# Attention and a squared-ReLU MLP on one core: the moving operand of both MLP products read as two interleaved halves

## The chip, the core and the metric

The kernel runs on one core of a Trainium2 chip. The metric is device time in microseconds (us) of one execution, lower is better. A core has TensorE (PE, matrix products, with its weight loads shown apart as PEld), VectorE (DVE), ScalarE (ACT), GpSimd (POOL), SyncE (SP, here the issuer of nearly all DMAs), an on-chip memory of 128 partitions (SBUF), and the accumulator memory that TensorE writes (PSUM).

## The reference

Causal attention over a window of 128 positions with a linear bias per head, for 8 batches, 8 heads, 576 positions and a head size of 64. Its output, 4608 tokens of 512 features, goes through a two-layer mixture with squared ReLU:

```python
scores = scale * np.matmul(q, k.transpose(0, 1, 3, 2))
scores = np.where(mask, scores + bias[None], -1000000000.0)
attn = softmax(scores)                       # window of 128, causal
x = np.matmul(attn, v).transpose(0, 2, 1, 3).reshape(4608, 512)
h = np.maximum(x @ w_in, 0.0)                # w_in  512 x 2048
out = (h * h) @ w_out                        # w_out 2048 x 512
```

Inputs and outputs are float32.

## The kernel before

**Tiles.** The 4608 tokens are worked on in 9 chunks (`NCH`) of 512. Everything is held transposed: features in the 128 partitions, the chunk's 512 tokens in the columns. The hidden layer's 2048 features are 16 blocks (`NF`) of 128.

**Precision.** Products run in fp32r, a four-byte type of fewer significant bits, and each float32 operand is split into a high and a low part. A product is three matmuls: high weight by high data, high weight by low data, low weight by high data.

**First product, `gemm1(c, f)`, L202.** For chunk c and hidden block f it accumulates 4 input blocks by 3 parts, 12 matmuls of 128 x 128 weights by 512 columns, into one PSUM bank `g`. The moving operand is `xs[cc][:, part]`: a row of 512 words of the tile `xu` ([128, 2, 512], high and low parts), which attention wrote. Then ACT takes the ReLU out of PSUM (L212), DVE (in chunk 0 mostly ACT) squares it (L215, L217), ACT rounds it to the high part `hh` (L219), and DVE subtracts to get the low part `hl` (L221). `hh` and `hl` are [128, 512] each.

**Second product, `gemm2(c, f)`, L231.** For hidden block f it adds to the four accumulators `acc` (one per 128 output features) 3 matmuls each, 12 in all, with `hh` and `hl` as moving operands. After the last f the accumulators are copied (L237) and stored (L238) to a transposed output [512, 4608], which the host transposes back.

**Weights.** They stay in SBUF for the whole run. Each high and low word lie side by side (`self.w[f]` is [128, 2, 512, 2]), so the 128 columns of a weight block are read 8 bytes apart. For the first product, in the blocks f = 0, 4, 8, 12 and there in the first two of the four input blocks (`APART`, L39 and L188), the columns are read 16 bytes apart instead; those are 6 of the 12 loads of such a group.

**Order.** From chunk 1 on, a written-out loop (L811 to L834) alternates one `gemm1` and, two hidden blocks behind, one `gemm2`; every eight half-steps the matmuls of the next pair of attention heads (`visit`, L541 and L548) come in between. The order on PE is the program's own. In the start and chunk 0 a planner (`Plan`) orders all engines. Before the first products PE also runs matmuls of zeros in bf16 (L129), whose result nobody uses.

Of the kernel before, what the change touches and what calls it, by code (L numbers as in the profile page):

```python
# [19 lines left out]
B, H, S, D = 8, 8, 576, 64  # L20
NP = H // 2
DM, DF = 512, 2048
NF = DF // 128
NCC = DM // 128
NCH = B * S // 512
# [31 lines left out]

def slope(h):
    return 2.0 ** (-8.0 * (h + 1) / H)


class Kern:
# [131 lines left out]
    def gemm1(self, c, f):  # L194
        nc = self.nc
        xs = [self.x[c, p] for p in range(NP)]
        g = self.big.tile([128, 2, 512], F32, name="g")[:, 1] if self.big else self.g1.tile([128, 512], F32, name="g")
        i = 0
        for cc in range(NCC):
            wl, wh = self.block(0, f, cc)  # L200
            for w, part in ((wh, 0), (wh, 1), (wl, 0)):
                nc.tensor.matmul(g, w, xs[cc][:, part], start=i == 0, stop=i == 11)  # L202
                i += 1
                if (c, f, i) == (0, 0, 9):
                    yield
        yield
        r = self.hp.tile([128, 512], F32, name="r", bufs=1)
        hh = self.hp.tile([128, 512], F32R, name="hh")
        hl = self.hp.tile([128, 512], F32R, name="hl")
        self.h[c, f] = hh, hl  # L210
        with self.tc.high_priority(offset=100):
            self.relu = nc.scalar.activation(r, g, AF.Relu)  # L212
        yield
        if c or f in SQUARES:
            nc.vector.tensor_tensor(r, r, r, op=ALU.mult)  # L215
        else:
            nc.scalar.activation(r, r, AF.Square)  # L217
        yield
        nc.scalar.copy(hh, r)  # L219
        yield  # L220
        nc.vector.tensor_tensor(hl, r, hh.bitcast(F32), op=ALU.subtract)  # L221

    def gemm2(self, c, f):
        nc = self.nc
        hh, hl = self.h.pop((c, f))
        if f == 0:
            self.acc = self.start_banks if c == 0 else [self.ac.tile([128, 512], F32, name="acc") for _ in range(4)]
        for m in range(4):
            wl, wh = self.block(1, f, m)
            for i, (w, h) in enumerate(((wh, hh), (wh, hl), (wl, hh))):  # L230
                nc.tensor.matmul(  # L231
                    self.acc[m], w, h, start=(f == 0 and i == 0), stop=(f == NF - 1 and i == 2)
                )
            if f == NF - 1:
                o = self.op.tile([128, 512], F32, name="o")
                out = self.outd[m * 128 : m * 128 + 128, 512 * c : 512 * c + 512]
                (nc.scalar.copy if m % 2 else nc.vector.tensor_copy)(o, self.acc[m])  # L237
                (nc.scalar if c == NCH - 1 and m == 3 else nc.sync).dma_start(out, o)  # L238
# [598 lines left out]
def _consts():  # L837
    r = np.arange(128)
    own, h = r % 64, (r // 64)[:, None]
    cst = np.zeros((128, CST), np.float32)  # L840
    cst[:, 0:128] = np.eye(128)
    keep = own[:, None] >= np.arange(64)[None, :]
    cst[:, 128:192] = np.where(h == 0, keep, ~keep).astype(np.int32).view(np.float32)
    cst[:, 192:256] = NEG
    rel = r[:, None] - r[None, :]
    rel = np.where(rel >= 0, rel, rel + 128)
    for a in range(H):
        cst[:, 256 + 128 * a : 384 + 128 * a] = -rel * (8 * slope(a))
    later = r[:, None] < r[None, :]
    near = [cst[:, 256 + 128 * a : 384 + 128 * a] for a in range(H)]  # L850
    return np.concatenate([cst] + [np.where(late, t, np.float32(NEG)) for t in near for late in (later, ~later)], axis=1)
# [40 lines left out]
```

## Time and profile before

| what | value |
|---|---|
| median of 3 runs (lowest to highest) | 941.89 us (941.58 to 941.97) |
| the profiled execution's span, first to last instruction | 939.1 us |
| matmuls of L202 / L231 | 1728 / 1728 |
| mean latency of one such matmul | 394 / 393 to 396 ns |
| DMA traffic over the span | 95.26 MB, mean 101 GB/s |

The page of a profile lists the busy time of each engine, a strip of 40 equal slices of the span (a digit is the busy share in tenths; PEclk is the granted TensorE clock), the chain of work that ended last followed back from the last instruction, and the costliest groups of instructions. A row of the groups reads: line, engine, operation, out<-in by the program's names, shape, count, then busy time in us and mean ns of one, then the idle time ahead of them and who ended it. A row of the timeline reads: start in us, length in us, engine, line, operation, and the count of instructions merged into it. A row of one line's view has minimum/median/maximum in ns. Matmuls are pipelined and overlap one another, so the length of one is not what it adds to the span.

### The profile page before, as it was taken

The numbers are of one execution on the slowest core, as the hardware profiler recorded it, in microseconds if no ns is written. First come the engines' busy times: TensorE is split into PE (matmuls) and PEld (weight loads), VectorE is DVE, ScalarE is ACT, GpSimd is POOL, SyncE is SP. The second block draws the span as 40 slices with busy tenths as digits, with TensorE's granted clock in tenths as the row PEclk, the third lists the DMA queues.
The fourth block names the chain that finished last, engine by engine and source line by source line (L and its number), as shares of the span: only waits on it lengthen the run. The fifth ranks groups of instructions, "written<-read, shape, count | busy, mean of one in ns | idle before, by whom it ended". The sixth has DMA issues, their size and how long they took to land.

```text
span 939.1 us, 19485 instructions
## 1 busy us (share of the span) xinstructions
PE 929.3 (99%) x7492; PEld 782.5 (83%) x7492; DVE 497.2 (53%) x1326; ACT 418.9 (45%) x1115; POOL 214.2 (23%) x255
## 2 busy tenths in 40 slices
PE   8899999999999999999999999999999999999998
PEld 5688888888888888888888888888888888888886
DVE  5999874445554555544555444455455454433222
ACT  7898753343444444334434343344444444322222
POOL 4223331222221222222222222221221222220000
PEclk9999999999999999999999999999999999999999
DMA  9975424222432233222423233334322231111001
GB/s 344 403 284 167 135 74 130 71 62 83 129 86 85 78 104 107 64 84 79 125 86 86 73 106 82 86 85 127 88 77 83 75 93 43 38 46 45 1 0 45
DMA packets 72893, 95.26 MB, mean 101 GB/s; under 512 B 8032, under 2 KB 41952, under 8 KB 72800
## 3 DMA queue, kind: packets, MB, share of 16 engines
q1 hardware_dynamic: 72368, 93.36, 32.6%
q8 instruction: 59, 0.97, 0.4%
q10 hardware_dynamic: 432, 0.66, 0.2%
q14 instruction: 34, 0.28, 0.1%
HBM read 67.76 MB, written 26.21 MB: 100 GB/s over the span
## 4 chain that ended last, share of the span: by engine, by line
PE 94%; DMA 3%; DVE 1%; ACT 1%; issue 0%; SPq 0%; POOLq 0%; DVEq 0%
PE acc L231 43%; PE g L202 42%; PE s L541 5%; PE g L548 2%; DMA raw<-in_dram 2%; PE s L548 1%; DMA wide<-in_dram 1%; PE at L346 1%; ACT t L470 0%; PE s L412 0%; PE at L412 0%; DVE t L482 0%; DVE tw L613 0%; DVE pp L629 0%; DVE raw L175 0%
## 5 line engine op out<-in xcount | busy, mean ns | idle before, releaser
L202 PE MATMUL g<-xu,w 128*128 128x512 f32 x1728 | 423.9, 394 | 1.4 <-issue 0.8
L202 PEld LDWEIGHTS g<-xu,w 128*128 128x128 f32 x1728 | 344.6, 209 | 56.7 <-issue 1.7
L231 PE MATMUL acc<-hh,w 128*128 128x512 f32 x1152 | 385.6, 396 | 0.0
L231 PEld LDWEIGHTS acc<-hh,w 128*128 128x128 f32 x1152 | 224.0, 194 | 45.5 <-issue 5.3
L212 ACT ACTIVATE r<-g 128x512 f32<-128x512 f32 x144 | 86.1, 598 | 353.2 <-PE g L202 353.1
L215 DVE TENSOR_TENSOR r<-r 128x512 f32<-128x512 f32 x129 | 91.9, 713 | 255.8 <-ACT r L212 255.8
L231 PE MATMUL acc<-hl,w 128*128 128x512 f32 x576 | 226.2, 393 | 0.0
L334 POOL TENSOR_SCALAR_AFFINE_SELECT pp<-pp 128x512 f32<-128x512 f32 x128 | 112.5, 879 | 215.6 <-DMA pp<-way 139.4
L221 DVE TENSOR_TENSOR hl<-r,hh 128x512 fp32r<-128x512 f32 x144 | 117.6, 816 | 74.4 <-ACT hh L219 71.9
L270 POOL TENSOR_TENSOR t<-t,nm 128x512 f32<-128x512 f32 x64 | 76.1, 1190 | 262.0 <-DVE nm L267 231.4
L231 PEld LDWEIGHTS acc<-hl,w 128*128 128x128 f32 x576 | 112.1, 195 | 19.6
L219 ACT CAST hh<-r 128x512 fp32r<-128x512 f32 x144 | 89.2, 619 | 78.0 <-DVE r L215 76.4
L259 ACT ACTIVATE t<-t,nm 128x128 f32<-128x128 f32 x256 | 100.1, 394 | 11.8 <-DVE nm L252 11.7
L321 DVE STREAM_TRANSPOSE pp<-t 128x512 f32<-128x512 f32 x64 | 45.2, 707 | 47.0 <-POOL t L270 39.5
L252 DVE CUSTOM_DVE_ANT_0 t<-t,cst 128x128 f32<-128x128 f32 x256 | 59.5, 295 | 1.0
L541 PE MATMUL s<-pp,v 64*64 64x128 f32 (+1 forms) x1792 | 52.0, 248 | 0.1
L541 PEld LDWEIGHTS s<-pp,v 64*64 64x64 f32 x1792 | 40.5, 134 | 10.4 <-issue 10.0
L259 ACT ACTIVATION_READ_ACCUMULATOR t<-t,nm 128x1 f32 x256 | 48.6, 190 | 0.0
L482 DVE COPY_PREDICATED t<-cst,s 64x256 f32<-64x256 int32 x100 | 44.4, 444 | 6.0 <-ACT t L463 3.1
L472 POOL MEMSET t<- 64x128 f32 (+1 forms) x44 | 10.0, 228 | 117.8 <-PE s L548 110.5
L529 ACT CAST xu<-s 128x512 fp32r<-128x512 f32 x28 | 16.4, 587 | 41.6 <-DVE t L482 26.6
L470 ACT COPY t<-g 64x256 f32<-64x256 f32 (+2 forms) x86 | 28.0, 340 | 3.8 <-PE g L548 1.0
(71 smaller groups left out, 482.3 us busy)
## 6 DMA issues: line engine op xcount, KB each, us to landing
raw<-in_dram SPq DMA_DIRECT2D x32, 512.0 KB, 8.7
way<-pp SPq DMA_DIRECT2D x256, 64.0 KB, 2.0
pp<-way SPq DMA_DIRECT2D x64, 256.0 KB, 2.8
qk<-in_dram SPq DMA_DIRECT2D x32, 320.0 KB, 3.2
v<-in_dram SPq DMA_DIRECT2D x32, 320.0 KB, 3.9
qk<-in_dram SPq DMA_DIRECT2D x38, 256.0 KB, 4.3
out_dram<-o SPq DMA_DIRECT2D x35, 256.0 KB, 2.6
v<-in_dram SPq DMA_DIRECT2D x3, 256.0 KB, 5.2
```

The costliest lines, as they stand in the source:

```text
L202: nc.tensor.matmul(g, w, xs[cc][:, part], start=i == 0, stop=i == 11)
L212: self.relu = nc.scalar.activation(r, g, AF.Relu)
L215: nc.vector.tensor_tensor(r, r, r, op=ALU.mult)
L219: nc.scalar.copy(hh, r)
L221: nc.vector.tensor_tensor(hl, r, hh.bitcast(F32), op=ALU.subtract)
L231: nc.tensor.matmul(self.acc[m], w, h, start=(f == 0 and i == 0), stop=(f == NF - 1 and i == 2))
L252: self.nc.vector.tensor_tensor_reduce(self.t[:, m], self.t[:, m], self.K.nrel(2 * self.p + m // 2), -0.125, BIG, ALU.add, ALU.min, self.nm ...
L259: return self.nc.scalar.activation(self.t[:, m], self.t[:, m], AF.Exp, bias=nm[:, m : m + 1], scale=-1.0, accum_out=nm[:, 4 + m : 5 + m],)
L270: self.nc.gpsimd.tensor_tensor(self.t, self.t, self.nm[:, 8:12].unsqueeze(2).to_broadcast([128, 4, 128]), op=ALU.mult)
L321: nc.vector.transpose(squares.rearrange("p b m c -> p m b c"), self.t.rearrange("p m (b c) -> p m b c", c=32))
L334: nc.gpsimd.affine_select(to, self.own, pattern=[[-32 * sign, 4], [0, 4], [-sign, 32]], compare_op=op, fill=0.0, base=0, channel_multiplie ...
L541: made.append(mm(to, w, x, start=first and n < 2, stop=not first, skip_group_check=True))
```

## The change

A helper `in_turn` gives a view of a row of 512 words in which its two halves come in turn: word 0, word 256, word 1, word 257, and so on. Both products read their moving operand through it. The result of a matmul is written to PSUM in contiguous order as before, so its column 2b + a holds what was column 256a + b. The tokens of a chunk are thus permuted once by the first product and once more by the second, and the host undoes the permutation twice after the run.

The instructions of every engine, their number, shapes and order, stay as they were; the access pattern of the moving operand in the two matmul lines is what differs.

```diff
+def in_turn(x):
+    return x.rearrange("p (a b) -> p b a", a=2)
...
-                nc.tensor.matmul(g, w, xs[cc][:, part], start=i == 0, stop=i == 11)
+                nc.tensor.matmul(g, w, in_turn(xs[cc][:, part]), start=i == 0, stop=i == 11)
...
                 nc.tensor.matmul(
-                    self.acc[m], w, h, start=(f == 0 and i == 0), stop=(f == NF - 1 and i == 2)
+                    self.acc[m], w, in_turn(h), start=(f == 0 and i == 0), stop=(f == NF - 1 and i == 2)
                 )
...
-    return np.ascontiguousarray(r.results[0]["out_0_dram"].T)
+    out = r.results[0]["out_0_dram"].T
+    for _ in range(2):
+        out = out.reshape(NCH, 256, 2, DM).transpose(0, 2, 1, 3).reshape(B * S, DM)
+    return np.ascontiguousarray(out)
```

## The prediction

> **What bounds the kernel now.** I read the page's busy times first, then the chain of work that ended last, then the costliest groups, and last the timeline of single matmul groups.
>
> ```profile
> span 939.1 us, 19485 instructions
> PE 929.3 (99%) x7492; PEld 782.5 (83%) x7492; DVE 497.2 (53%) x1326; ACT 418.9 (45%) x1115; POOL 214.2 (23%) x255
> PEclk9999999999999999999999999999999999999999
> PE 94%; DMA 3%; DVE 1%; ACT 1%; issue 0%; SPq 0%; POOLq 0%; DVEq 0%
> PE acc L231 43%; PE g L202 42%; PE s L541 5%; PE g L548 2%; DMA raw<-in_dram 2%; PE s L548 1%; DMA wide<-in_dram 1%; PE at L346 1%; ACT t L470 0%; PE s L412 0%; PE at L412 0%; DVE t L482 0%; DVE tw L613 0%; DVE pp L629 0%; DVE raw L175 0%
> L202 PE MATMUL g<-xu,w 128*128 128x512 f32 x1728 | 423.9, 394 | 1.4 <-issue 0.8
> L231 PE MATMUL acc<-hh,w 128*128 128x512 f32 x1152 | 385.6, 396 | 0.0
> L231 PE MATMUL acc<-hl,w 128*128 128x512 f32 x576 | 226.2, 393 | 0.0
> ```
>
> TensorE is busy for 929.3 of 939.1 us, the clock is granted in full throughout, and the two lines that the change edits hold 85% of the chain. They issue 1728 + 1152 + 576 = 3456 matmuls of 512 columns. The mean of one, 394 ns, is a latency; matmuls overlap, so the price is the pitch from one start to the next. I take it from a stretch in which both products alternate without a gap:
>
> ```profile
> 902.05 2.92 PE L202 MATMUL g<-xu,w 128*128 128x512 f32 x12
> 904.81 0.39 PE L231 MATMUL acc<-hh,w 128*128 128x512 f32 x1
> ...
> 907.58 2.97 PE L202 MATMUL g<-xu,w 128*128 128x512 f32 x12
> 910.38 0.39 PE L231 MATMUL acc<-hh,w 128*128 128x512 f32 x1
> ```
>
> Twelve matmuls take 904.81 − 902.05 = 2.76 us, a pitch of **0.230 us**. The second group takes 2.80 us; it is one of the 36 groups (f divisible by 4, nine chunks) whose first six weight loads come through the strided blocks of L188. The other 288 − 36 = 252 groups are plain. So the two products fill 252 × 2.76 + 36 × 2.80 = 796.3 us, and 939.1 − 796.3 = 142.8 us of the span is something else (the start, attention's matmuls between the groups, the last copy and store). The median of the timed runs, 941.89 us, is 2.8 us above this profile's span; I add these 2.8 us at the end.
>
> Whether longer matmuls are absorbed anywhere is seen in the windows by stage:
>
> ```profile
> 0.00:43.00 43.00, 38.46 (x380) 24.83 (x380) 31.38 (x110) 35.09 (x103) 15.07 (x20) 1.00 0.98 371
> 43.00:140.00 97.00, 96.17 (x646) 80.79 (x641) 85.66 (x189) 75.89 (x170) 31.54 (x34) 1.00 0.54 176
> 140.00:905.00 765.00, 764.31 (x6342) 651.35 (x6341) 371.82 (x1017) 300.65 (x831) 167.58 (x201) 1.00 0.28 80
> 905.00:939.10 34.10, 30.38 (x132) 25.52 (x131) 8.30 (x12) 7.26 (x12) 0.00 (x0) 1.00 0.08 31
> ```
>
> The first number after the length is PE. From 43 us, where the products are under way, to 905 us PE idles 0.83 + 0.69 us, about 1.5 us in all. There is nothing to absorb a longer pitch: what one matmul gains or loses is paid 3456 times, on the path.
>
> **The change, part by part.** No instruction is added, removed or moved on any engine, no DMA, and no wait. The relu, square, cast and subtract between the products run over contiguous 512-word rows as before; that their columns mean other tokens costs them nothing, and the host's reordering is outside the metric. Nothing changes in the weight loads, and PSUM is written in the same contiguous order. The whole change is the order in which TensorE reads its moving operand: today word 0, 1, 2, ... of a row, afterwards word 0, 256, 1, 257, ..., so no two words read in succession are neighbours; they lie 1024 bytes apart. The sum has one unknown, the pitch p of such a matmul: time = 142.8 + 2.8 + 3456 × p.
>
> No matmul of this trace streams a strided moving operand, so p must be bounded from the nearest rows. Those are weight loads, which read SBUF too, in three spacings:
>
> ```profile
> L581 PEld LDWEIGHTS acc<-qk x24: 182/186/187, 6.4 to 15.1; 64*128 64x128 f32 x24
> L299 PEld LDWEIGHTS acc<-pp,v x84: 132/137/137, 16.6 to 30.7; 128*64 128x64 f32 x84
> L202 PEld LDWEIGHTS g<-xu,w x12: 193/194/197, 901.8 to 904.4; 128*128 128x128 f32 x12
> ...
> L202 PEld LDWEIGHTS g<-xu,w x12: 193/252/312, 907.3 to 909.9; 128*128 128x128 f32 x12
> ```
>
> The columns are minimum/median/maximum in ns. 128 neighbouring words take 186 (L581), 64 take 137 (L299): (186 − 137)/64 = 0.77 ns a word and 186 − 128 × 0.77 = 88 ns fixed. Words 8 bytes apart (L202, plain group: high and low parts lie in pairs) take 194, hardly more. Words 16 bytes apart, in the six strided loads of the group at 907, take 312. So two words within 16 bytes still come at the contiguous price, and a word alone in its 16 bytes costs (312 − 88)/128 = **1.75 ns**. (L581 and L299 load plain fp32, L202 fp32r; the type is not separated from the spacing there. Between L202's own two spacings it is.)
>
> The moving stream today costs 230/512 = 0.449 ns a word, that is 4 × 0.449 = 1.80 ns for each 16 bytes. That is nearly the 1.75 ns that a lone word costs the weight reader: both rows look like a reader that spends about 1.75 to 1.80 ns on each 16-byte piece, however many words it uses of it. The changed stream uses one word of a piece and goes to another. I take the mean, 1.77 ns: p = 512 × 1.77 = 0.906 us, and the time is 145.6 + 3456 × 0.906 = 145.6 + 3131 = **3277 us**.
>
> Bounds of this case: a lone word at two contiguous slots, 2 × 0.77 = 1.54 ns, gives p = 0.788 and 2869 us. Above, in the strided group six matmuls share 2.80 − 6 × 0.230 = 1.42 us, 0.237 us for one load of 128 lone words if the load sets that pitch, so 1.85 ns a word: p = 0.947, 3418 us.
>
> [...]
>
> What else becomes late: nothing. At 3.5 times the length, DVE's 497.2 us and ACT's 418.9 us shrink to 15% and 13% of the span, and the copy and store behind the last matmul stay. If PE's clock fell because the array stands waiting, the matmuls outside the two products would suffer: PE's 929.3 − 796.3 = 133 us at half the clock would add at most 133 us, about 3410 us, still in the case's bounds.
>
> **The rivals.**
> *A word price instead of a piece price.* The moving reader may open a piece faster than the weight reader, and lose only the pairing of neighbours. For it: the moving stream today (0.449 ns a word) is faster than the weight reader's 0.77, so it isn't simply the same reader. Doubling 0.449 gives p = 0.460 and 145.6 + 1590 = 1735 us. Ends: a word at the weight reader's contiguous price, 0.77 ns, gives p = 0.394 and 1508 us; the lone word's surcharge (312 − 194)/128 = 0.92 ns on top of today's 0.449 gives p = 0.701 and 2569 us. Against it: the near equality of 1.75 and 1.80 would then be chance.
>
> *The new order costs nothing.* If the reader keeps two pieces open, or fetches far enough ahead, words 0, 256, 1, 257 use both pieces fully, and p stays 0.230: the change would not do what it says to the memory, and the time stays within 938 to 946 us. For it: PE's pace elsewhere is set by columns, and only weight loads show a spacing price. Against it: the strided loads' neighbouring pieces would gain from fetching ahead too, and they do not.
> [...]
>
> *Faster.* The trace has a shorter stream of 512 columns: the bf16 matmuls that keep the array warm.
>
> ```profile
> 7.50 0.60 PE L129 MATMUL g<-zero 128*128 128x512 bf16 x2
> ...
> L129 PE MATMUL g<-zero x32: 376/379/634, 1.3 to 32.8; 128*128 128x512 bf16 x32
> ```
>
> Two of them take 0.60 us, one 0.379, so their pitch is about 0.22 us, where the products have 0.230. If those 0.010 to 0.014 us are the four-byte words of one piece waiting for each other, and alternate pieces free them, 3456 × 0.012 = 41 us go: about 900 us. It decides only if two pieces are held open at once, so it needs the second rival and one thing more. Against it: the type differs too, which explains the gap as well.
>
> **How the numbers follow.** The piece price 0.50 (2869 to 3418, likeliest 3277); the word price and what lies up to the surcharge 0.31 (1508 to 2569); no cost 0.15; faster 0.04. Leaving out the last two, 0.19, the range is **1508 to 3420**; the first case's own is 2869 to 3418. A measurement of this kernel tells about 0.2% from no change; by the cases, faster 0.04, within 0.2% 0.15, slower 0.81.
>
> **What would show it.** The pitch of L202's and L231's successors decides: a group of twelve at about 10.9 us is the piece price, 5.5 us the word price, 2.76 us no cost. Plain weight loads should still take 194 ns and strided ones 312, the granted clock stay full, and the attention matmuls' groups between the products keep their length. The prediction is wrong if the pitch is below 0.79 us; it is wrong in kind if the pitch is right and PE now waits for another engine.

## The result: 941.74 to 903.59 us

The changed kernel takes 903.59 us (median of 4, 903.36 to 904.06) against 941.74 us for the kernel before (median of 4 runs): a ratio of 0.96, 95% interval 0.9587 to 0.9614. It is **faster by 38 us**. The prediction had 3277 us and a range from 1508; its rival "faster", with 900 us, had been given a chance of 0.04.

From the page of the changed kernel (the lines of the code stand four further down):

```profile
span 901.8 us, 19481 instructions
PE 885.8 (98%) x7488; PEld 791.5 (88%) x7492; DVE 507.8 (56%) x1326; ACT 426.4 (47%) x1115; POOL 209.4 (23%) x255
...
PE 86%; DVE 8%; ACT 3%; issue 2%; DMA 1%; SPq 0%; DVEq 0%; ACTq 0%; POOLq 0%
PE acc L235 38%; PE g L206 38%; PE s L545 5%; PE g L552 2%; DVE w L185 2%; DVE raw L181 2%; ACT tw L602 1%; PE s L552 1%; DVE raw L179 1%; DVE t L486 1%; DMA qk<-in_dram 1%; DVE hl L225 0%; ACT t L474 0%; PE g L133 0%; DVE t L256 0%
...
L206 PE MATMUL g<-xu,w 128*128 128x512 f32 x1728 | 404.8, 384 | 6.7 <-ACT r L216 4.1
```

TensorE still bounds the kernel. Two things are new in the chain: DVE holds 8% of it instead of 1%, the weight conversions L179, L181 and L185 alone 5%, and the first product waits 4.1 us for ACT. The timeline of the same stretch late in the run gives the pitch:

```profile
866.56 2.75 PE L206 MATMUL g<-xu,w 128*128 128x512 f32 x12
869.15 0.38 PE L235 MATMUL acc<-hh,w 128*128 128x512 f32 x1
...
871.74 2.88 PE L206 MATMUL g<-xu,w 128*128 128x512 f32 x12
874.46 0.38 PE L235 MATMUL acc<-hh,w 128*128 128x512 f32 x1
```

Twelve matmuls of a plain group take 869.15 − 866.56 = 2.59 us, a pitch of **0.216 us** instead of 0.230. The group with six strided weight loads takes 2.72 us instead of 2.80, so its first six matmuls are at (2.72 − 6 × 0.216)/6 = 0.237 us, as they were before.

By the pitch, 252 plain groups gain 0.17 us each and 36 strided ones 0.08 us: 42.8 + 2.9 = 46 us. The spans differ by 37.3. The rest went in the start: the tenth group of the first product begins at 96.43 us now and at 90.99 us in the kernel before, although the shorter pitch gains from the first group on. The windows show over half of this as idle time of PE. The first row below is the kernel before, the second the changed one (length, then the busy time of PE, PEld, DVE, ACT and POOL, then granted clock, DMA share and GB/s).

```profile
43.00:95.00 52.00, 51.17 (x353) 42.86 (x349) 49.61 (x109) 47.08 (x95) 14.16 (x16) 1.00 0.67 234
```

```profile
43.00:95.00 52.00, 46.32 (x283) 39.90 (x273) 50.55 (x92) 49.23 (x88) 17.93 (x14) 0.97 0.66 232
```

Between 43 and 95 us PE idled 0.83 us before and idles 5.68 us now, while DVE and ACT are nearly full. In this execution the granted clock, the third number from the end, falls from 1.00 to 0.97: behind a wait of 2.28 us for ACT it is 0.50 between 89 and 91 us, and the group from 87.88 to 92.38 us takes 4.50 us; but the two timed runs with a mean clock of 1.00 took 903.36 and 904.06 us, so the total does not hang on the clock. The work of DVE and ACT there is the conversion of the weights, and its steps take longer. Before, then after (count | busy us, mean ns):

```profile
L173 ACT ACTIVATE raw<-raw 128x1024 f32<-128x1024 f32 x16 | 18.2, 1160 | 0.3 <-DMA raw<-in_dram 0.2
L179 ACT CAST w<-raw 128x1024 fp32r<-128x1024 f32 x13 | 15.0, 1160 | 3.8 <-DVE raw L177 3.6
```

```profile
L177 ACT ACTIVATE raw<-raw 128x1024 f32<-128x1024 f32 x16 | 21.0, 1355 | 0.0
L183 ACT CAST w<-raw 128x1024 fp32r<-128x1024 f32 x13 | 20.2, 1565 | 4.9 <-DVE raw L181 4.7
```

The same instruction on the same data takes 17% longer in the one line and 35% in the other. So the changed kernel differs in two ways: the moving stream is faster, and the conversions that run beside it are slower. The last experiments look into the second.

### The profile page after: what moved, and what is told of

Same layout as the page of the kernel before. It is cut to its first block, busy times and chain, and to the rows that moved or that the text cites. A ratio compares the mean times of both kernels' runs of the same rounds, so it can differ in the third digit from the quotient of the medians.

```text
span 901.8 us, 19481 instructions
## 1 busy us (share of the span) xinstructions
PE 885.8 (98%) x7488; PEld 791.5 (88%) x7492; DVE 507.8 (56%) x1326; ACT 426.4 (47%) x1115; POOL 209.4 (23%) x255
## 4 chain that ended last, share of the span: by engine, by line
PE 86%; DVE 8%; ACT 3%; issue 2%; DMA 1%; SPq 0%; DVEq 0%; ACTq 0%; POOLq 0%
PE acc L235 38%; PE g L206 38%; PE s L545 5%; PE g L552 2%; DVE w L185 2%; DVE raw L181 2%; ACT tw L602 1%; PE s L552 1%; DVE raw L179 1%; DVE t L486 1%; DMA qk<-in_dram 1%; DVE hl L225 0%; ACT t L474 0%; PE g L133 0%; DVE t L256 0%
## 5 line engine op out<-in xcount | busy, mean ns | idle before, releaser
L206 PE MATMUL g<-xu,w 128*128 128x512 f32 x1728 | 404.8, 384 | 6.7 <-ACT r L216 4.1
L206 PEld LDWEIGHTS g<-xu,w 128*128 128x128 f32 x1728 | 349.0, 214 | 39.4 <-ACT r L216 5.3
L235 PE MATMUL acc<-hh,w 128*128 128x512 f32 x1152 | 369.3, 382 | 0.0
L235 PEld LDWEIGHTS acc<-hh,w 128*128 128x128 f32 x1152 | 226.4, 197 | 26.6 <-issue 5.3
L235 PE MATMUL acc<-hl,w 128*128 128x512 f32 x576 | 218.3, 379 | 0.0
L219 DVE TENSOR_TENSOR r<-r 128x512 f32<-128x512 f32 x129 | 88.3, 685 | 226.7 <-ACT r L216 226.4
L225 DVE TENSOR_TENSOR hl<-r,hh 128x512 fp32r<-128x512 f32 x144 | 124.4, 864 | 74.9 <-ACT hh L223 74.8
L274 POOL TENSOR_TENSOR t<-t,nm 128x512 f32<-128x512 f32 x64 | 70.3, 1099 | 255.9 <-DVE nm L271 206.1
```

The costliest lines, as they stand in the source:

```text
L206: nc.tensor.matmul(g, w, in_turn(xs[cc][:, part]), start=i == 0, stop=i == 11)
L235: nc.tensor.matmul(self.acc[m], w, in_turn(h), start=(f == 0 and i == 0), stop=(f == NF - 1 and i == 2))
L274: self.nc.gpsimd.tensor_tensor(self.t, self.t, self.nm[:, 8:12].unsqueeze(2).to_broadcast([128, 4, 128]), op=ALU.mult)
```

## The experiments

Every kernel below but e1, g1 and e7 differs from the changed kernel only in the order in which the 512 words of a row are read, and in the host's reordering that belongs to it. The pitch is that of plain groups, taken from two starts in the timeline as above; the two products' lines stand a few lines further down in each. A 16-byte piece is four neighbouring words, a unit that the prediction took from the weight loads (194 ns with words 8 bytes apart, 312 with 16). A time without a range is that of one run.

### Is it the neighbourhood of words, and does a lone word cost what a weight load pays?

```diff
 def in_turn(x):
-    return x.rearrange("p (a b) -> p b a", a=2)
+    return x.rearrange("p (a b) -> p b a", a=256)     # e2_step8:  0, 2, 4, ... then 1, 3, 5, ...
+    return x.rearrange("p (a b) -> p b a", a=128)     # e3_step16: 0, 4, 8, ...
+    return x.rearrange("p (a b c) -> p b a c", a=2, c=2)  # e4_pairs: 0, 1, 256, 257, 2, 3, ...
```

> Both products read every second word (0, 2, 4, ..., then 1, 3, 5, ...): successive words are 8 bytes apart, two of each 16-byte piece. Theory A (successive words that are direct neighbours in memory cost the moving reader a little, and any other order is free): pitch 0.216 us in plain groups as in the changed kernel, time about 903. Theory B (an opened 16-byte piece costs about 1.75 ns unless an earlier one is still open): two words a piece, 256 pieces twice over, pitch about 0.45 us, time about 1700. Theory C (two words of one piece in a row cost a little, 14 ns in all for the 512): pitch still about 0.230, time about 942.

> Both products read every fourth word (0, 4, 8, ...): each word alone in its 16-byte piece, and the piece comes back only 128 words later. Theory A: pitch 0.216 us, time about 903. Theory B: pitch about 0.90 us, as the forecast had it, time about 3270; the changed kernel would have escaped it only because two pieces stay open. Theory C: no two words of a piece in a row, so 0.216 and about 903 as A.

> Both products take the two halves in turn by pairs of words (0, 1, 256, 257, 2, 3, ...). Theory A and C: half of the neighbourly steps are left, pitch between 0.216 and 0.230, about 0.223, time about 922. Theory D (the moving reader takes two words in one go only where they are aligned neighbours, and that step is what costs): pitch 0.230, time about 942.

Measured: 1708.41, 1740.61 and 1286.05 us. The timeline of e3_step16:

```profile
1701.68 5.76 PE L209 MATMUL g<-xu,w 128*128 128x512 f32 x12
1707.24 0.66 PE L238 MATMUL acc<-hh,w 128*128 128x512 f32 x1
```

That is (1707.24 − 1701.68)/12 = 0.463 us: a word alone in its 16 bytes costs 0.90 ns on the moving side, not the 1.77 the prediction had carried over from the weight loads. The pitches of the other two are 0.453 and 0.327. Theories A and C fell on all three, D on e4. B's 0.45 for e2 came true, but its 0.90 for e3 did not. Nothing yet says why the halves are fast.

### Are the 14 ns a collision with the weight loads?

```diff
-        if APART(i, f, b):
-            w = w.rearrange("p (n j o) t -> p n o j t", n=2, o=2)[:, b // 2, b % 2]
-        else:
-            w = w[:, 128 * b : 128 * b + 128]
-        return w[..., 0], w[..., 1]
+        w = w.rearrange("p d t -> p (d t)")[:, 256 * b : 256 * b + 256]
+        return w[:, 128:256], w[:, 0:128]
```

together with the old order of the moving operand (`in_turn` returns its argument) and no load 16 bytes apart. The weights are then high and low words of other features, so this kernel computes another product; the number, shapes and order of its instructions stay.

> Moving operand in the old order; the weight loads take 128 neighbouring words instead of every second or fourth, so that each load touches 32 pieces of 16 bytes, not 64 or 128 (its columns are then high and low words of other features, and the product is another one). Theory A, C, D (the 14 ns belong to the moving reader alone): pitch stays 0.230, time 940 to 942. Theory E (they are collisions of the moving reads with those of the weight load): fewer pieces, fewer collisions, pitch about 0.222, time about 915.

Measured: 949.68 us.

```profile
910.47 2.96 PE L206 MATMUL g<-xu,w 128*128 128x512 f32 x12
913.27 0.40 PE L235 MATMUL acc<-hh,w 128*128 128x512 f32 x1
```

The pitch is (913.27 − 910.47)/12 = 0.233 us, longer than with the wider-spaced loads. E fell. But the claim that the loads have no part in it did not hold either: with loads of neighbouring words the pitch is 3 ns longer, in the direction nobody expected.

### Does the distance decide, or the number of streams?

```diff
-    return x.rearrange("p (a b) -> p b a", a=2)
+    return x.rearrange("p (a b) -> p b a", a=4)       # f4_quarters: 0, 128, 256, 384, 1, ...
+    return x.rearrange("p (a b) -> p b a", a=16)      # f16_sixteenths
+    return x.rearrange("p (a b) -> p b a", a=64)      # f64_step32
+    return x.rearrange("p (a b c) -> p b a c", a=2, c=4)  # q4_pieces_in_turn: 0 to 3, 256 to 259, ...
```

> Both products read four quarters in turn (0, 128, 256, 384, 1, ...): successive words 512 bytes apart. Known so far: 1024 bytes apart 0.216 us a matmul, 8 bytes apart 0.453, 16 bytes apart 0.462, pairs of halves 0.327. Theory F (two successive words are fetched at once when they lie in different parts of the memory, and distance decides): 0.216 if 512 bytes still mean different parts, else about 0.45. Theory G (the reader keeps two pieces open and no more): four streams don't fit, every word opens its piece anew, about 0.46 and 1740 us.

> Both products read sixteen parts in turn, successive words 128 bytes apart. Theory F: 0.216 or about 0.45, a step somewhere between 1024 and 16 bytes; no value between. Theory G: about 0.46, 1740 us.

> Both products read sixty-four parts in turn, successive words 32 bytes apart. Theory F: 0.216 if neighbouring pairs of pieces lie in different parts of the memory, else about 0.45. Theory G: about 0.46, 1740 us.

> Both products take the two halves in turn by four words, a whole 16-byte piece at a time (0 to 3, 256 to 259, 4 to 7, ...). Theory H (what made pairs of halves slow, 0.327 against 0.216, is the third loop of the access pattern: about 0.86 ns at each of its 128 turns): 64 turns, 0.216 + 0.055 = 0.271, time about 1090. Theory F without a price for the third loop: at most the contiguous 0.230, time about 942.

Measured: 1088.02, 1651.68, 1632.67 and 1001.05 us. The timeline of f4_quarters:

```profile
1049.63 3.44 PE L209 MATMUL g<-xu,w 128*128 128x512 f32 x12
1052.91 0.44 PE L238 MATMUL acc<-hh,w 128*128 128x512 f32 x1
```

Quarters have a pitch of 0.273, between F's 0.216 and 0.45 and far below G's 0.46. The others stand at 0.437, 0.432 and 0.247. The first two lie near F's 0.45 and G's 0.46 alike; for the last F had at most 0.230 and H had 0.271. So neither distance nor the number of open pieces alone fits, and the third loop has no such price.

The excess over 0.216 has a form, though: 57 ns for quarters, 111 for pairs, 216 to 247 for e2, e3, f16 and f64, which come back to a piece only 16 to 255 words later (e2 after two of its words in succession). Those are about 64, 128 and 256 times 0.84 to 0.96 ns, and 0.216 us is itself 256 times 0.84 ns. That is how theory K came up, an estimate from these pitches alone: that the words are taken two at a time, and that the first of each two and the second go through readers of their own. No run shows such readers, and K's step, put at about 0.83 ns in the expectations below, is an estimate from the same pitches.

### Theory K against the rest

```diff
-    return x.rearrange("p (a b) -> p b a", a=2)
+    return x.rearrange("p (n a b) -> p n b a", a=2, b=4)  # e6_next_piece: 0, 4, 1, 5, 2, 6, 3, 7, 8, ...
+    return x.rearrange("p (n a b) -> p n b a", a=2, b=2)  # e5_in_piece: 0, 2, 1, 3, 4, 6, 5, 7, ...
```

> Both products take two neighbouring 16-byte pieces in turn, word by word (0, 4, 1, 5, 2, 6, 3, 7, 8, 12, ...). Theory K (words are taken two at a time; the first and the second of each two go through readers of their own, each holding its 16-byte pieces; a new piece costs one step of about 0.83 ns unless its reader took at least two words in a row from the piece before): each reader takes four in a row (0 to 3, and 4 to 7), as with the halves, so 0.216 us a matmul and about 903, although the words are only 16 bytes apart. Theory F (successive words must lie 1024 bytes apart): 0.43 to 0.46, 1630 to 1740. Theory H (a turn of the third loop costs 0.86 ns): 0.271, 1090.

> Both products read 0, 2, 1, 3, 4, 6, 5, 7, ...: the order within each 16-byte piece is changed, the order of the pieces is not. Theory K: each reader takes two in a row from a piece (0, 1 and 2, 3), as in the contiguous order: 0.230, about 942. Theory A (direct neighbours cost): 0.216, about 903. Theory H: 0.216 + 128 x 0.86 ns = 0.326, about 1280.

Measured: 895.21 and 941.69 us. First e6, then e5:

```profile
853.11 2.75 PE L209 MATMUL g<-xu,w 128*128 128x512 f32 x12
855.70 0.38 PE L238 MATMUL acc<-hh,w 128*128 128x512 f32 x1
```

```profile
902.86 2.92 PE L209 MATMUL g<-xu,w 128*128 128x512 f32 x12
905.62 0.39 PE L238 MATMUL acc<-hh,w 128*128 128x512 f32 x1
```

2.59/12 = 0.216 and 2.76/12 = 0.230, both as K said, where F and H were far off and A fell on e5. The order that alternates between neighbouring 16-byte pieces is as quick as the one over 1024 bytes; the order that changes places within a piece alone does nothing. All thirteen orders, with the pieces that every second word comes from, the first, third, fifth and so on, which theory K gives to one reader (a letter is a 16-byte piece):

| order | pieces of every second word | new pieces among these 256 words | pitch, us |
|---|---|---|---|
| halves in turn (the change) | A A A A B B B B | 64 | 0.216 |
| neighbouring pieces in turn (e6) | A A A A B B B B | 64 | 0.216 |
| 32 or 512 bytes apart (g3, g2, below) | A A A A B B B B | 64 | 0.216 |
| contiguous (before) | A A B B | 128 | 0.230 |
| within the piece (e5) | A A B B | 128 | 0.230 |
| pieces of the halves in turn (q4) | A A B B | 128 | 0.247 |
| quarters (f4) | A B A B A B A B | 64 | 0.273 |
| pairs of the halves (e4) | A B A B C D C D | 128 | 0.327 |
| 32, 128, 8, 16 bytes apart (f64, f16, e2, e3) | A B C D | 256 | 0.432 to 0.463 |

With four of these words in a row from a piece the pitch is 0.216 us; with two in a row it is 0.230 or 0.247; where the pieces change with each of these words, it lies above 0.216 by 0.84 to 0.96 ns for each new piece, and going back to the piece used one of these words earlier adds nothing to that. This last clause was read off e4 and f4; e5, e6, g2 and g3 were forecast with the rest of K. K as recorded lets a new piece cost nothing after two words in a row, which by itself would put the contiguous order at 0.216; its 0.230 for e5 was carried over from the contiguous order.

### One product alone, and the strided weight loads

```diff
-                    self.acc[m], w, in_turn(h), start=(f == 0 and i == 0), stop=(f == NF - 1 and i == 2)
+                    self.acc[m], w, in_turn2(h), start=(f == 0 and i == 0), stop=(f == NF - 1 and i == 2)
...
+def in_turn2(x):                                       # e8_first_only
+    return x
```

> Only the first product reads the halves in turn, the second reads its operands in the old order. If the gain belongs to each matmul by itself: first product 0.216, second 0.230, and about half of the gain of 38 us, so about 922. If it comes from something that both must share (the order of tokens, the start), it is far from the middle.

Measured: 921.93 us, half of the gain; the first product's plain groups are at 0.216, the second's at 0.231. The effect belongs to each product by itself.

```diff
-APART = lambda i, f, b: i == 0 and f % 4 == 0 and b < 2
+APART = lambda i, f, b: False                          # e1_loads_alike, on the halves in turn
```

> The changed kernel with every weight load 8 bytes apart, none 16 bytes apart. In the changed kernel's trace the 216 matmuls behind a strided load have a pitch of about 0.236 against 0.216, so 216 x 0.020 = 4.4 us should go: about 899. If the 16-byte loads are hidden, or their waits move elsewhere, it stays at 903.6.

Measured: 899.82 us (899.60 to 900.61), a ratio to before of 0.9562, interval 0.9546 to 0.9578; 3.8 us below the changed kernel where 4.4 were expected. The strided loads, which before nearly hid behind a pitch of 0.230 (2.80 us a group against 2.76), now cost their groups 2.72 us against 2.59.

### What slowed the conversions, and the best kernel

e6 has the pitch of the changed kernel and the same instructions in the same order on every engine, yet is 8.4 us faster. Its conversions are at the old length, so I varied the distance alone:

```diff
-    return x.rearrange("p (a b) -> p b a", a=2)
+    return x.rearrange("p (n a b) -> p n b a", a=2, b=128)  # g2_apart512
+    return x.rearrange("p (n a b) -> p n b a", a=2, b=8)    # g3_apart32
```

> Within each half of 256 words, its two halves in turn: successive words 512 bytes apart. Theory K: pitch 0.216 (each reader takes four in a row from a piece). Conversions: if a distance of exactly 1024 bytes is what slows them, ACT's first step stays at 1.16 us and the time is about 895; if any two distant places do, it is near 1.36 us and the time about 903.

> Within each 16 words, the two halves of 8 in turn: successive words 32 bytes apart. Theory K: pitch 0.216. Conversions at 1.16 us and about 895 if only distant places slow them; were the next piece's own readiness what made the neighbouring pieces cheap for the others, something between 895 and 903.

Measured: 902.68 and 894.46 us, both with a pitch of 0.216. ACT's first conversion step in e6 (16 bytes), g2 (512 bytes) and g3 (32 bytes), minimum/median/maximum in ns:

```profile
L180 ACT ACTIVATE raw<-raw x16: 1111/1158/1213, 25.1 to 88.7; 128x1024 f32<-128x1024 f32 x16
```

```profile
L180 ACT ACTIVATE raw<-raw x16: 1147/1418/1821, 24.3 to 95.0; 128x1024 f32<-128x1024 f32 x16
```

```profile
L180 ACT ACTIVATE raw<-raw x16: 1092/1166/1234, 24.6 to 88.7; 128x1024 f32<-128x1024 f32 x16
```

With the two places 16 or 32 bytes apart ACT keeps its 1160 ns; in the mean it takes 1431 at 512 bytes and 1355 at 1024 bytes, so it is not 1024 bytes as such. The last of these sixteen steps begins at 95 us instead of 89 (the last two times of a row). The tenth group of the first product begins at 96.43 us in the changed kernel and at 89.09 us in e6, so 7.3 of the 8.3 us between their spans are lost by then.

The distance alone does not decide it, though. Here is the same step in f4_quarters, whose successive words lie 512 bytes apart too, and in q4_pieces_in_turn, which takes four neighbouring words before it changes the half:

```profile
L180 ACT ACTIVATE raw<-raw x16: 1111/1168/1237, 25.1 to 96.8; 128x1024 f32<-128x1024 f32 x16
```

```profile
L180 ACT ACTIVATE raw<-raw x16: 1131/1510/1885, 25.4 to 98.0; 128x1024 f32<-128x1024 f32 x16
```

Quarters, at a pitch of 0.273, leave the step as it was; whole pieces of the halves, at 0.247, lengthen it most. Which property of the order or of its pace does it stays open.

```diff
-APART = lambda i, f, b: i == 0 and f % 4 == 0 and b < 2
+APART = lambda i, f, b: False
...
-    return x.rearrange("p (a b) -> p b a", a=2)
+    return x.rearrange("p (n a b) -> p n b a", a=2, b=4)    # g1_next_piece_alike
```

> Neighbouring pieces in turn (0, 4, 1, 5, ...) and every weight load 8 bytes apart. In the trace with strided loads the 216 matmuls behind them have a pitch of 0.233 to 0.234 against 0.216, so 216 x 0.018 = 3.9 us go from 895.2: about 891.3. Theory that the two share a cause (loads and stream collide): less than 2 us, above 893.

Measured: **892.26 us** (891.90 to 892.33), a ratio to before of 0.9479, interval 0.9466 to 0.9491. The two gains add up but for a microsecond: 2.95 us went from e6's 895.21, which is a single time. Against e1, which has the same loads and reads 1024 bytes apart, the neighbouring pieces save 899.82 − 892.26 = 7.6 us, with several runs on both sides.

## Why the prediction was wrong

**The bound was right.** The two products' pitch times 3456 was the term that moved, and nothing absorbs a loss there: with e3's pitch of 0.463 us the prediction's sum gives 145.6 + 3456 × 0.463 = 1746 us, and e3 took 1740.61.

**The price of a lone word was wrong, and it is the step that failed first.** The prediction took 1.75 ns from the weight loads and 1.80 ns for 16 bytes of the moving stream, and read their nearness as one mechanism: "both rows look like a reader that spends about 1.75 to 1.80 ns on each 16-byte piece". e3_step16 measures lone words on the moving side: 0.463 us a matmul, 0.90 ns a word. The rival with a price per word had 0.460 us and 1735 us, close to what e3 took. The nearness of 1.75 and 1.80 was no sign of one mechanism.

**The second failure decided the sign: the changed order is no order of lone words.** The prediction reasoned "the changed stream uses one word of a piece and goes to another", as if going away meant losing the piece. In the halves order all four words of both pieces are used within eight words, and the pitch is 0.216 us; the orders that come back to a piece only 16 to 255 words later (e2, e3, f16, f64) take 0.432 to 0.463. The rival "the new order costs nothing" had named two ways, two pieces kept open or fetching ahead. The argument against it, that the strided loads would gain too, bears on fetching ahead alone; those loads never come back to a piece, so they could not speak against pieces kept open.

**The rival "faster" had the size.** It took the shorter stream of the bf16 matmuls, about 0.22 us (the first eight of the trace took 3.95 us, later pairs 0.60), for what the fp32r stream could reach, and came to about 900 us; the pitch is 0.216. Its condition, two pieces held open, fits the runs. Its reason does not: it had words of one piece wait for one another, while the quick orders of the table are those in which every second word takes more words of a piece in a row, four (0.216) instead of two (0.230). So the 900 us came in part by luck. The argument that held it down to 0.04, that the type explains the gap, is refuted: the type is the same in the halves order, fp32r, and 2.59/12 us is the pitch now where 2.76/12 was before.

**"What else becomes late: nothing" was wrong.** The conversions got longer by the change itself, which the prediction had not considered, since no other engine's instruction is touched. PE idled 5.68 − 0.83 = 4.9 us more between 43 and 95 us, while e6, with the same instructions and the old conversion lengths, idles 0.99 us there. The strided weight loads, which the prediction had kept at 312 ns, took 338 in the group at 871.74; the plain ones of that group stayed at 194. ACT's 1160 ns became 1355 and 1565 while PE read 1024 bytes apart. The half clock that the prediction named did occur, 0.50 between 89 and 91 us, but behind a wait of PE for ACT; under the slow stream of e3, 0.463 us a matmul, the mean granted clock was 0.998.

**The range** left out both cases in which the time does not rise, with 0.19. The profile had no row of a strided moving operand, and one analogy between two engine parts carried half of the chance.

## What to carry to other kernels

Where fp32r matmuls with 512 columns run back to back at 0.230 us, read the moving operand so that successive words come in turn from two neighbouring 16-byte pieces (0, 4, 1, 5, ...); it costs a view and a permutation of the columns, and brought 0.216 here. Keep the two places close to one another (16 or 32 bytes here), and look at the lengths of the other engines' unchanged instructions afterwards: they can grow, as the conversions' did. And look again at what was hidden behind the old pitch, here the strided weight loads.

## What the runs showed of the hardware that was not expected

- The order of reading changes a matmul of 512 fp32r columns between 0.216 and 0.463 us, with contiguous reading (0.230) not the fastest.
- A spacing of 8 bytes, nearly free for weight loads (194 ns, against 186 for the neighbouring words of L581 in the kernel before), doubles the pitch of the moving stream (0.453 us against 0.230).
- ACT and DVE, working in place on 8-byte steps, took longer beside orders that alternate between places 512 or 1024 bytes apart at 0.216 to 0.247 us a matmul, and not at 16 or 32 bytes, nor beside the quarters at 0.273: in the changed kernel DVE's second conversion step (L181) rises from 1350 to 1621 ns. The ACT steps on attention's tiles, such as L259 of before at 394 ns, do not change.
- Open: why the orders with two words of a piece in a row lie above 0.216 us, by 14 ns when contiguous and by 31 ns when the pieces of two halves alternate; why weight loads of neighbouring words lengthen the old order's pitch from 0.230 to 0.233; and which property of an order makes the conversions longer. The two readers of theory K are an estimate from the pitches of the orders tried; no run shows them.
